# Seven block products for the feed-forward of two batches: attention and feed-forward on one Trainium2 core

## The chip, the core and the metric

The program runs on one core of one Trainium2 chip. A core has a matmul engine (PE in the profile; its weight loads PEld), a vector engine (DVE), a scalar engine (ACT), GpSimd (POOL) and a sequencer (SP) that issues the transfers here. The metric is device microseconds of one execution, lower is better. The kernel before takes 623.44 us, median of three runs (622.62 to 623.99).

## What is computed

Four batches of twelve heads, 448 positions of 64 values. Attention with capped scores, then two matrices with a gate between:

```
scores = cap * tanh((q @ k.T / 8) / cap);  attn = softmax(scores);  o = attn @ v
x = o.transpose(0, 2, 1, 3).reshape(1792, 768)
h = x @ w_in                                                  # 768 x 2048, float64 weights
g = where(h >= 1, h, where(h <= -1, 0, (h + 1)**2 / 4))
out = g @ w_out                                               # 2048 x 768
```

## The kernel before

`fast_body` holds the whole work; `general_body` behind it runs only if a verdict on the data's ranges, computed on the device, asks for it. Everything is kept transposed: model dimension on the 128 partitions, the 448 positions of one batch along the free axis.

A head pair (`attention(n)`, n from 0 to 23, six to a batch) is one unit of attention: `split` cuts q and k into two half-precision parts, `qk` multiplies the scores in three half-precision products, `expo` takes tanh and exp on the scalar engine, `add` sums exponentials on the vector engine, `av` multiplies with the values, `norm` and `divide` divide by the sums. For pairs 0 to 11 `av` runs in float32 (L444). For pairs from `HALVED` = 12 on, `halve` and `halve_v` (L385, L386, L391, L340) cut exponentials and values into two half-precision parts, and `av` runs three half-precision products (L433). How many of the four chunks of exponentials the vector engine sums and how many go to the matmul engine (L465) is `direct(n)`.

The feed-forward of a batch is two layers of 128x448 tiles. Layer one has 16 tiles of 6 chunks (`h_mm`, L537 to L539), layer two 6 tiles of 16 chunks (`o_mm`, L566 to L568). Each chunk is three half-precision matmuls: high weight by high data, low by high, high by low. Between the layers `h_out` applies the gate: two scalar-engine operations (L549, L550), a clamp on the vector engine (L551), and the cut into high and low half (L554, L555). The float64 weights come in 28 pieces; `piece` decodes each on the vector engine through one of two buffers `z` (L281 to L283) into float32 and then into two halves (L284 to L286). `piece_check` reads all pieces once more during batches 1 to 3 and reduces their largest and smallest magnitude (L297) for the verdict.

The order of all instructions is made at build time by `Plan`: every step is added with the buffers that it reads and writes, its possible engines and a cost; `order` then lists the steps on each engine by lateness in a planned schedule. The engines run their queues in that order and wait on semaphores. The steps of later attention pairs get a lead (`AHEAD`) and are planned among the feed-forward of the batches before; those of batch 3 lie among the feed-forward of batches 1 and 2.

## Time and profile before

| | |
|---|---|
| median of the runs | 623.44 us |
| the profiled execution, its time | 623.54 us |
| its span, first to last instruction | 621.7 us |
| PE busy | 607.5 us, 98% of the span |
| DVE busy | 427.8 us, 69% |
| ACT busy | 398.2 us, 64% |
| granted PE clock, mean | 0.997 of 2.4 GHz |
| moved by DMA | 74.6 MB, 120 GB/s on average |

Busy time is the time in which at least one instruction of an engine runs. Matmuls overlap each other, so the mean duration of one in a list is longer than the distance of two starts; the same holds, to a smaller degree, of the vector and the scalar engine. The granted clock is a share of 2.4 GHz; the lower of its two levels is 1.2 GHz. In the lists a group names line, engine, operation, what it writes and reads, its shape, then how often it occurs, its busy time in us and the mean ns of one, and behind the bar the engine's idle time before it and what ended that.

### The profile page before, as it was taken

How to read it: one execution, taken by the hardware profiler on the slowest of the kernel's cores; microseconds unless marked ns; L12 is line 12 of the kernel's file. 1: busy time of each engine (PE TensorE's matmuls, PEld its weight loads, DVE VectorE, ACT ScalarE, POOL GpSimd, SP SyncE). 2: the span in 40 equal slices, each digit the busy share in tenths (PEclk: the TensorE clock that was granted, in tenths of full speed). 3: DMA queues.
4: the chain of work that ended last, by engine and by line, in shares of the span. 5: the costliest groups of instructions: out<-in, count | busy, mean ns of one | idle time of the engine just before them, and what ended most of it. 6: DMA issues, size and time to landing. Idle time of an engine off the chain costs nothing.

```text
span 621.7 us, 8987 instructions
## 1 busy us (share of the span) xinstructions
PE 607.5 (98%) x3626; PEld 288.5 (46%) x3626; DVE 427.8 (69%) x673; ACT 398.2 (64%) x576; POOL 1.2 (0%) x6
## 2 busy tenths in 40 slices
PE   8998999999999999999999999999999999999995
PEld 2333454434445444444454444444545555555552
DVE  6997999999999569898875447888842105654200
ACT  7998977999845579897776459879622115551000
...
GB/s 344 310 260 167 185 67 179 172 142 169 199 208 97 98 33 113 107 133 117 152 116 129 65 40 52 58 102 74 129 134 31 15 31 102 101 137 146 36 16 34
DMA packets 18629, 74.60 MB, mean 120 GB/s; under 512 B 2066, under 2 KB 5266, under 8 KB 15506
## 3 DMA queue, kind: packets, MB, share of 16 engines
...
q14 instruction: 21, 0.17, 0.1%
q10 hardware_dynamic: 2, 0.00, 0.0%
...
## 4 chain that ended last, share of the span: by engine, by line
PE 71%; ACT 14%; DVE 11%; issue 2%; DMA 1%; POOL 0%; SPq 0%; DVEq 0%; ACTq 0%; POOLq 0%
PE f L566 12%; PE f L567 12%; PE f L568 12%; PE f L537 7%; PE f L538 7%; PE f L539 7%; PE s L367 5%; ACT e L375 4%; ACT e L377 4%; PE av L433 4%; PE av L444 2%; PE t L465 1%; DVE wr L551 1%; DVE spl L340 1%; DVE z L282 1%
## 5 line engine op out<-in xcount | busy, mean ns | idle before, releaser
L537 PE MATMUL f<-x,w 128*128 128x448 f16 x384 | 135.5, 353 | 1.5 <-DVE wr L551 1.5
L566 PE MATMUL f<-g,w 128*128 128x448 f16 x384 | 135.5, 353 | 0.1
L568 PE MATMUL f<-g,w 128*128 128x448 f16 x384 | 135.3, 352 | 0.0
L539 PE MATMUL f<-x,w 128*128 128x448 f16 x384 | 135.3, 352 | 0.0
L567 PE MATMUL f<-g,w 128*128 128x448 f16 x384 | 135.3, 352 | 0.0
L538 PE MATMUL f<-x,w 128*128 128x448 f16 x384 | 135.3, 352 | 0.0
L375 ACT ACTIVATE e<-s,tsc 128x896 f32<-128x896 f32 (+1 forms) x96 | 84.8, 902 | 9.6 <-PE s L367 8.6
L573 ACT ACTIVATE wr<-f 128x448 f32<-128x448 f32 x24 | 12.9, 538 | 100.3 <-PE f L568 100.3
L367 PE MATMUL s<-spl 64*128 64x448 f16 (+1 forms) x504 | 66.3, 352 | 0.6 <-DVE low L618 0.5
L297 DVE TENSOR_REDUCE chk<-raw 128x1 f32<-128x768 f32 (+1 forms) x56 | 58.0, 1060 | 10.9 <-DMA raw<-w_out 9.9
L537 PEld LDWEIGHTS <-w 128*128 128x128 f16 x384 | 37.5, 98 | 38.1 <-issue 4.4
L549 ACT ACTIVATE r<-f,half 128x448 f32<-128x448 f32 x64 | 40.2, 627 | 22.5 <-PE f L539 22.4
L554 ACT ACTIVATE g<-wr 128x448 f16<-128x448 f32 x64 | 36.6, 572 | 27.9 <-DVE wr L551 27.7
L566 PEld LDWEIGHTS <-w 128*128 128x128 f16 x384 | 37.5, 98 | 36.3 <-issue 2.2
L538 PEld LDWEIGHTS <-w 128*128 128x128 f16 x384 | 37.6, 98 | 35.7 <-issue 2.1
L568 PEld LDWEIGHTS <-w 128*128 128x128 f16 x384 | 37.6, 98 | 35.1
L539 PEld LDWEIGHTS <-w 128*128 128x128 f16 x384 | 37.6, 98 | 35.1
L567 PEld LDWEIGHTS <-w 128*128 128x128 f16 x384 | 37.6, 98 | 34.4 <-issue 0.3
L551 DVE SCALAR_TENSOR_TENSOR wr<-f,r 128x448 f32<-128x448 f32 x64 | 39.5, 619 | 18.2 <-ACT r L550 17.4
L377 ACT ACTIVATE e<-e,lnes,capb 128x896 f32<-128x896 f32 (+1 forms) x48 | 48.4, 1037 | 0.6
L555 DVE SCALAR_TENSOR_TENSOR g<-wr,g 128x448 f16<-128x448 f32 x64 | 39.4, 618 | 11.7 <-ACT g L554 11.4
L444 PE MATMUL av<-e,vt 128*64 128x448 f32 (+1 forms) x168 | 44.4, 562 | 1.0 <-ACT e L377 1.0
...
## 6 DMA issues: line engine op xcount, KB each, us to landing
...
vt<-vp SPq DMA_DIRECT2D x24, 256.0 KB, 3.1
...
```

The source lines that it names most:

```text
L297: dve(width, lambda j=j, op=op: V.tensor_reduce(out=chk[:, j:j + 1], in_=hi, op=op, axis=AX.X, apply_absolute_value=True), rk + after, [(" ...
L367: T.matmul(s[:, j, :S], lhsT=t[h, a, S + c * P:S + (c + 1) * P], rhs=t[h, b, :S], start=(i == 0), stop=(i == 2))
L375: act(w * S + 60, lambda: A.activation(e[:, :w], s[:, :w, :S], AF.Tanh, scale=tsc), sk + [("tsc", None)], ek)
L377: act(w * S + 110, lambda: A.activation(e[:, :w], e[:, :w], AF.Exp, scale=capb, **bias), ek + [("tsc", None)], ek)
L444: T.matmul(o, lhsT=w, rhs=m, start=(c == 0), stop=(c == 3))
L537: T.matmul(ph, lhsT=w1[:, 0, fc, c], rhs=x[c][0][:, 0], start=(c == 0), stop=False)
L538: T.matmul(ph, lhsT=w1[:, 1, fc, c], rhs=x[c][0][:, 0], start=False, stop=False)
L539: T.matmul(ph, lhsT=w1[:, 0, fc, c], rhs=x[c][0][:, 1], start=False, stop=(c == NCC - 1))
L551: dve(S, lambda: V.scalar_tensor_tensor(out=w, in0=ph, scalar=WS * XS, in1=r, op0=ALU.max, op1=ALU.min), fk + rk, wk)
L566: T.matmul(po, lhsT=hi[:, fc], rhs=gv[:, 0], start=(fc == 0), stop=False)
L567: T.matmul(po, lhsT=lo[:, fc], rhs=gv[:, 0], start=False, stop=False)
L568: T.matmul(po, lhsT=hi[:, fc], rhs=gv[:, 1], start=False, stop=(fc == NFC - 1))
```

## The change

The last two batches are taken together as two block columns of the data, and each layer's weights as 2x2 blocks (chunks by tiles). Both layers are multiplied with seven block products instead of eight (Strassen's scheme in its form with fifteen sums). For that:

- `attention` of all pairs comes before the two batches' feed-forward; pairs 18 to 23 (the last batch) use float32 values in `av` and are no longer halved.
- Decoded weights are kept in memory (`zd`); attended values of batches 2 and 3 (`xd`) and gated values of both batches (`gd`) are stored there in float32 and read back.
- `pair_up` loads four blocks and makes four differences, `halves_of` cuts each into two half-precision parts: 3 groups for layer one, 8 for layer two.
- `weights_sum` makes four sums of weight blocks, `weights_split` cuts them: 8 times for layer one (384 columns wide), 6 for layer two (512). Layer two's go over weights in place that are no longer needed.
- `product` is one block product; `copy_out` (scalar engine) and `plus` (vector engine) join products that two tiles share.
- The weight checks go through the `z` buffers in halves and are added to the plan behind the attention.

```diff
-HALVED = 2 * NPR
-ND = (B * NPR - HALVED) // 2
+HALVED = range(2 * NPR, 3 * NPR)
+PAIRED = 2 * NPR
+HF, HC, HE = NFC // 2, NCC // 2, NEC // 2
+STEP = 2
...
-WS, XS, GS, QS, ES = 2.0 ** 15, 2.0 ** 13, 4.0, 2.0 ** 10, 2.0 ** 5
+WS, XS, GS, QS, ES = 2.0 ** 13, 2.0 ** 13, 4.0, 2.0 ** 10, 2.0 ** 5
...
+    zd = [dr.tile([P, NCC * P if i < NP1 else NFC * EH], F32, name="zd%d" % i) for i in range(NT)]
+    xd = {n: dr.tile([P, S], F32, name="xd%d" % n) for n in range(PAIRED, B * NPR)}
+    gd = {(b, fc): dr.tile([P, S], F32, name="gd%d_%d" % (b, fc)) for b in (2, 3) for fc in range(NFC)}
...
+        dma(4 * P * width, lambda: M.dma_start(zd[i], z), zk, [("zd", i)])
...
-    def piece_check(i, after):
+    def piece_check(i, part):
 
         k = i - NP1
-        width = NCC * P if k < 0 else NFC * EH
-        t, rk = raws[6].bitcast(I32)[:, :2 * width], [(("w2", 6), None)]
+        width = (NCC * P if k < 0 else NFC * EH) // 2
+        zt, zk = take("z", zs)
+        t = zt.bitcast(I32)[:, :2 * width]
         hi = t.rearrange("p (n two) -> p n two", two=2)[:, :, 1].bitcast(F32)
-        src = w_in[i] if k < 0 else w_out[k]
-        dma(8 * P * width, lambda: M.dma_start(t, src.bitcast(I32)), [], rk)
-        for j, op in ((i, ALU.max), (NT + i, ALU.min)):
-            dve(width, lambda j=j, op=op: V.tensor_reduce(out=chk[:, j:j + 1], in_=hi, op=op, axis=AX.X, apply_absolute_value=True), rk + after, [("chk", j)])
+        src = (w_in[i] if k < 0 else w_out[k])[:, part * width:(part + 1) * width]
+        dma(8 * P * width, lambda: M.dma_start(t, src.bitcast(I32)), [], zk)
+        for j, op in ((0, ALU.max), (1, ALU.min)):
+            dve(width, lambda j=j, op=op: V.tensor_reduce(out=chp[:, j, i, part:part + 1], in_=hi, op=op, axis=AX.X, apply_absolute_value=True), zk, [("chp", (j, i, part))])
...
-            x, xk = st["x", n] = take_x()
-            xh, xl = [(xk, 0)], [(xk, 1)]
-            scale = XS if n < HALVED else 1.0
+            scale = 1.0 if n in HALVED else XS
             dve(S, lambda xf=xf, scale=scale: V.scalar_tensor_tensor(out=xf, in0=xf, scalar=scale, in1=t[:, :S], op0=ALU.mult, op1=ALU.mult), tk + fk, fk)
-            either(fk, xh, act_(S, lambda x=x, xf=xf: A.copy(x[:, 0], xf)), dve_(S, lambda x=x, xf=xf: V.tensor_copy(x[:, 0], xf), True))
-            left(S, x[:, 1], xf, 1.0, x[:, 0], FX + n, fk + xh, xl)
-
-    def take_x():
-
+            if n >= PAIRED:
+                dma(4 * P * S, lambda n=n, xf=xf: M.dma_start(xd[n], xf), fk, [("xd", n)])
+            if not 3 * NPR <= n < 3 * NPR + HC:
+                x, xk = st["x", n] = take_x(n)
+                halves_of(x, xk, xf, 1.0, fk, FX + n - (HC if n >= 3 * NPR else 0))
...
+    def halves_of(t, key, full, scale, r, j=None):
+
+        hk, lk = [(key, 0)], [(key, 1)]
+        cast = (lambda: A.copy(t[:, 0], full), lambda: V.tensor_copy(t[:, 0], full)) if scale == 1.0 else (lambda: A.activation(t[:, 0], full, AF.Copy, scale=scale), lambda: V.tensor_scalar(t[:, 0], full, scalar1=scale, scalar2=None, op0=ALU.mult))
+        either(r, hk, act_(S, cast[0]), dve_(S, cast[1], True))
+        if j is None:
+            dve(S, lambda: V.scalar_tensor_tensor(out=t[:, 1], in0=full, scalar=scale, in1=t[:, 0], op0=ALU.mult, op1=ALU.subtract), r + hk, lk)
+        else:
+            left(S, t[:, 1], full, scale, t[:, 0], j, r + hk, lk)
...
+    def gate(b, fc, src, key, dest, spill, keep):
+
+        (r, rk), (w, wk) = take("r", rs), dest
+        root = math.sqrt(GS)
+        acc = dict(accum_out=racc[:, b]) if fc == 0 else {}
+        act(S + (170 if acc else 0), lambda: A.activation(r, src, AF.Relu, bias=half, scale=0.5 * root / (WS * XS), **acc), key + [("half", None)], rk + [(("racc", b), fc)])
+        act(S, lambda: A.activation(r, r, AF.Square, scale=math.sqrt(WS * XS / GS)), rk, rk)
+        dve(S, lambda: V.scalar_tensor_tensor(out=w, in0=src, scalar=WS * XS, in1=r, op0=ALU.max, op1=ALU.min), key + rk, wk)
+        if spill:
+            dma(4 * P * S, lambda: M.dma_start(gd[b, fc], w), wk, [("gd", (b, fc))])
+        if keep is not None:
+            t, gk = st["g", b, fc] = keep
+            halves_of(t, gk, w, GS / (WS * XS), wk)
...
-    pieces = [lambda a, i=i: piece_check(i, a) for i in range(NT)]
-    checks = [(), pieces[::3], pieces[1::3], pieces[2::3]]
-    for b in range(B):
+    for b in range(2):
...
-        if b < B - 1:
-            for n in range(NPR):
-                plan.lead, plan.held = AHEAD * (b > 0), b > 0
-                attention((b + 1) * NPR + n)
-                plan.lead, plan.held = 0.0, False
+        for n in range((b + 1) * NPR, (b + 2 + b) * NPR):
+            plan.lead, plan.held = AHEAD[n // NPR - 1], b > 0
+            attention(n)
+            plan.lead, plan.held = 0.0, False
...
+    for i in range(NT):
+        for part in range(2):
+            piece_check(i, part)
...
+    def pair_up(srcs):
+
+        tiles = [take_from("xl", xl, xlk) for _ in srcs]
+        for (dram, dk), (t, k) in zip(srcs, tiles):
+            dma(4 * P * S, lambda t=t, dram=dram: M.dma_start(t, dram), [dk], k)
+        (a, ak), (d, dk), (e, ek), (b, bk) = tiles
+        less = lambda out, x, y, r, w: dve(S, lambda: V.tensor_tensor(out=out, in0=x, in1=y, op=ALU.subtract), r, w)
+        less(a, d, a, ak + dk, ak)
+        less(d, e, d, ek + dk, dk)
+        less(e, e, a, ek + ak, ek)
+        less(b, b, e, bk + ek, bk)
+        return [(a, ak), (e, ek), (d, dk), (b, bk)]
...
+    def product(bank, first, stop, lhs, rhs, r):
+
+        t, k = bank
+        n = len(rhs)
+
+        def run():
+            for c in range(n):
+                for i, (x, y) in enumerate(((0, 0), (1, 0), (0, 1))):
+                    T.matmul(t, lhsT=lhs(x, c), rhs=rhs[c][0][:, y], start=(first and c == i == 0), stop=(stop and c == n - 1 and i == 2), skip_group_check=True)
+        pe(567 * n, run, r + [(key, j) for _, key in rhs for j in range(2)] + ([] if first else k), k)
...
+    def weights_sum(a11, a12, a21, a22, keys, n):
+
+        k11, k12, k21, k22 = keys
+        tt = lambda out, x, y, op, r, w: dve(n, lambda: V.tensor_tensor(out=out, in0=x, in1=y, op=op), r, w)
+        tt(a22, a21, a22, ALU.add, k21 + k22, k22)
+        tt(a21, a11, a21, ALU.subtract, k11 + k21, k21)
+        tt(a11, a22, a11, ALU.subtract, k11 + k22, k11)
+        tt(a12, a12, a11, ALU.subtract, k11 + k12, k12)
+
+    def weights_split(n, hi, lo, full, r, hk, lk):
+        either(r, hk, act_(n, lambda: A.activation(hi, full, AF.Copy, scale=-WS)), dve_(n, lambda: V.tensor_scalar(hi, full, scalar1=-WS, scalar2=None, op0=ALU.mult), True))
+        dve(n, lambda: V.scalar_tensor_tensor(out=lo, in0=full, scalar=-WS, in1=hi, op0=ALU.mult, op1=ALU.subtract), r + hk, lk)
...
+    half1 = HC * P
+    for i in range(HF):
+        (za, zak), (zb, zbk) = take_from("zl", zl, zlk), take_from("zl", zl, zlk)
+        for t, k, src in ((za, zak, i), (zb, zbk, HF + i)):
+            dma(4 * P * NCC * P, lambda t=t, src=src: M.dma_start(t, zd[src]), [("zd", src)], k)
+        part = lambda k: [[(k[0][0], q)] for q in range(2)]
+        (k11, k12), (k21, k22) = part(zak), part(zbk)
+        weights_sum(za[:, :half1], za[:, half1:], zb[:, :half1], zb[:, half1:], (k11, k12, k21, k22), half1)
...
+        y, x, z = new_bank(), new_bank(), new_bank()
+        product(y, True, True, wl(i, 0), xb(PAIRED), wk(i))
+        p1 = copy_out(y)
+        product(x, True, True, wl(i, HC), xb(PAIRED + HC), wk(i))
+        plus(x, p1)
+        gate(2, i, *p1, p1, True, keep_g())
+        product(y, False, True, sl(sa, 0), tb(1), sak)
+        u2 = copy_out(y)
+        product(z, True, True, sl(sb_, 0), tb(2), sbk)
+        product(y, False, True, sl(sb_, HC), tb(0), sbk)
+        u4 = copy_out(y)
+        product(y, False, True, sl(sa, HC), xb(3 * NPR + HC), sak)
+        gate(3, i, *y, take_from("u", us, uk), True, None)
+        plus(z, u4)
+        gate(3, HF + i, *u4, u4, True, keep_g())
+        product(z, False, True, wl(HF + i, HC), tb(3), wk(HF + i))
+        plus(z, u2)
+        gate(2, HF + i, *u2, u2, True, keep_g())
...
+            if i < 4:
+                pair_g(done)
+                done += 1
...
+    p1s, u2s, u4s = [], [], []
+    for i in range(HE):
+        steps(ys[i], True, wv(i, 0), ga(2, 0), wqk(i, 0))
+        p1s.append(scaled(ys[i]))
+    for i in range(HE):
+        steps(xbs[i], True, wv(i, 1), ga(2, 1), wqk(i, 1))
+        plus(xbs[i], p1s[i], out_scale)
+        store(2, i, p1s[i])
+    while done < HF:
+        pair_g(done)
+        done += 1
...
+    for i in range(HE):
+        for h in range(2):
+            tiles = [take_from("zl2", zl2, zl2k) for _ in range(4)]
+            for q, (t, k) in enumerate(tiles):
+                src = zd[NP1 + 2 * (i + q // 2 * HE) + h][:, q % 2 * HF * EH:(q % 2 + 1) * HF * EH]
+                dma(4 * P * HF * EH, lambda t=t, src=src: M.dma_start(t, src), [("zd", NP1 + 2 * (i + q // 2 * HE) + h)], k)
+            weights_sum(*[t for t, _ in tiles], [k for _, k in tiles], HF * EH)
...
+            dests = [([s2v[i][j][:, :, e] for j in range(2)], ("s2", i))]
+            dests += [([w2_half(ec, j)[:, f * HF:(f + 1) * HF, e] for j in range(2)], ("wq", ec, f)) for ec, f in ((i, 1), (i, 0), (HE + i, 0))]
+            for (d, dk), (t, k) in zip(dests, tiles):
+                weights_split(HF * EH, d[0], d[1], t.rearrange("p (f e) -> p f e", e=EH), k, [(dk, (h, 0))], [(dk, (h, 1))])
+    for i in range(HE):
+        steps(wbs[i], True, wv(i, 1), ga(3, 1), wqk(i, 1))
+    for i in range(HE):
+        steps(ys[i], False, lambda x, c, i=i: s2v[i][x][:, c], gb(1), [(("s2", i), None)])
+        u2s.append(scaled(ys[i]))
+    for i in range(HE):
+        steps(ys[i], False, wv(HE + i, 0), gb(0), wqk(HE + i, 0))
+        u4s.append(scaled(ys[i]))
+        c12 = take_from("xl", xl, xlk)
+        plus(wbs[i], u4s[i], out_scale, c12)
+        store(3, i, c12)
+    for i in range(HE):
+        steps(zbs[i], True, wv(i, 0), gb(2), wqk(i, 0))
+        plus(zbs[i], u4s[i], out_scale)
+        store(3, HE + i, u4s[i])
+        steps(zbs[i], False, wv(HE + i, 1), gb(3), wqk(HE + i, 1))
+        plus(zbs[i], u2s[i], out_scale)
+        store(2, HE + i, u2s[i])
```

How the order moves, in three places. Names are the program's buffers: `t0` is the PSUM bank of sums, `rr0` their reciprocals, `e0` to `e4` exponentials and later weights, `xf` attended values, `eh0`, `vh0`, `vh1` the blocks of `pair_up`, `qkr`, `spl` q and k and later weight sums, `w2_2` layer-two weights of tile 2, `chk`, `chp` check results.

First place: the vector engine at the last reciprocal of the attention (pair 23). Before:

```order
L475 RECIPROCAL rr0_129<-t0_142 128x224
L386 TENSOR_TENSOR eh0_99<-e2_96,eh0_99 128x896
L478 SCALAR_TENSOR_TENSOR mix0_130<-mix0_130,low_73,rr0_129 128x224
L297 TENSOR_REDUCE chk_76<-raw_85 128x1 x2
L482 TENSOR_REDUCE chk_76<-rr0_129 128x1 x2
L386 TENSOR_TENSOR z0_86<-e3_97,z0_86 128x896
L494 SCALAR_TENSOR_TENSOR xf0_131<-xf0_131,t0_142 128x448
L386 TENSOR_TENSOR z1_87<-e4_98,z1_87 128x896
L340 SCALAR_TENSOR_TENSOR x1_106,fin_74<-xf0_131,x1_106 128x448
L386 TENSOR_TENSOR eh0_99<-e0_94,eh0_99 128x448
```

Now:

```order
L489 RECIPROCAL rr0_132<-t0_145 128x224
L307 TENSOR_REDUCE chp_80<-z1_90 128x1
L492 SCALAR_TENSOR_TENSOR mix0_133<-mix0_133,low_75,rr0_132 128x224
L307 TENSOR_REDUCE chp_80<-z1_90 128x1
L331 MEMSET rr0_132 1x71
L506 SCALAR_TENSOR_TENSOR xf0_134<-xf0_134,t0_145 128x448
L307 TENSOR_REDUCE chp_80<-z0_89 128x1
L354 SCALAR_TENSOR_TENSOR e0_97,fin_76<-eh0_102,e0_97 128x448
L354 SCALAR_TENSOR_TENSOR x1_109,fin_76<-xf0_134,x1_109 128x448
L354 SCALAR_TENSOR_TENSOR e0_97,fin_76<-vh1_104,e0_97 128x448
```

Between the reciprocal and the two attended values of the last pairs there were halves of exponentials; now there are halves of block differences (`e0`, from `eh0` and `vh1`) and weight checks, and the second attended value, `xf1`, stands 17 rows behind the first.

Second place: the vector engine some forty instructions later, at the third block group of layer one (`sums0` and `sums1` now hold halves of differences):

```order
L781 SCALAR_TENSOR_TENSOR spl1_94<-e4_101,spl1_94 128x768
L735 TENSOR_TENSOR eh0_102<-eh0_102 128x448
L773 TENSOR_TENSOR e3_100<-e3_100 128x384
L735 TENSOR_TENSOR eh0_102<-vh0_103,eh0_102 128x448
L354 SCALAR_TENSOR_TENSOR sums0_106,fin_76<-eh0_102,sums0_106 128x448
L735 TENSOR_TENSOR vh0_103<-vh0_103,eh0_102 128x448
L354 SCALAR_TENSOR_TENSOR sums1_107,fin_76<-eh0_102,sums1_107 128x448
L781 SCALAR_TENSOR_TENSOR spl0_93<-e3_100,spl0_93 128x768
```

and the matmul engine at the product that reads `sums1`:

```order
L758 LDWEIGHTS qkr1_92
L758 MATMUL s0_140<-e2_99,qkr1_92 128x448
L758 LDWEIGHTS qkr1_92
L758 MATMUL s0_140<-sums1_107,qkr1_92 128x448
L758 LDWEIGHTS qkr1_92
...
L758 LDWEIGHTS qkr0_91
L758 MATMUL f0_142<-x4_112,qkr0_91 128x448
```

This is the first product of a block difference. Nothing of it was in the old order, where the feed-forward of batch 3 needed batch 3 alone.

Third place: the vector engine at the last group of layer-two weight sums, where `w2_2` is written over:

```order
L773 TENSOR_TENSOR spl1_94<-spl0_93,spl1_94 128x512
L768 SCALAR_TENSOR_TENSOR xf1_135<-s1_141,xf1_135 128x448
L773 TENSOR_TENSOR spl0_93<-qkr0_91,spl0_93 128x512
L307 TENSOR_REDUCE chp_80<-z0_89 128x1
L773 TENSOR_TENSOR qkr0_91<-spl1_94,qkr0_91 128x512
L307 TENSOR_REDUCE chp_80<-z0_89 128x1
L773 TENSOR_TENSOR qkr1_92<-qkr1_92,qkr0_91 128x512
L307 TENSOR_REDUCE chp_80<-z1_90 128x1 x2
L781 SCALAR_TENSOR_TENSOR w2_2_84<-qkr1_92,w2_2_84 128x8x64
L781 SCALAR_TENSOR_TENSOR w1_81<-qkr0_91,w1_81 128x8x64
L781 SCALAR_TENSOR_TENSOR w2_5_87<-spl1_94,w2_5_87 128x8x64
```

and the matmul engine at the product that reads the new `w2_2` into bank `s0`, the third tile of that block product:

```order
L758 LDWEIGHTS w2_4_86
L758 MATMUL f1_143<-raw_88,w2_4_86 128x448
L758 LDWEIGHTS w2_4_86
L758 MATMUL f1_143<-raw_88,w2_4_86 128x448
L758 LDWEIGHTS w2_2_84
L758 MATMUL s0_140<-g16_131,w2_2_84 128x448
```

In the old order weights were written once, in the first third of the program; now the second layer's are written again while its products run.

## Rows read from the trace of the kernel before

**Rows 1.** Windows of stretches: busy us (instructions) of each engine, granted clock, DMA share.

```profile
core 0: us, PE busy (x) PEld busy (x) DVE busy (x) ACT busy (x) POOL busy (x), PEclk, DMA share, GB/s
62.00:200.00 138.00, 137.63 (x826) 63.19 (x826) 134.61 (x184) 114.25 (x161) 0.00 (x0) 1.00 0.46 159
200.00:424.00 224.00, 222.23 (x1368) 107.66 (x1366) 164.98 (x244) 168.56 (x244) 0.00 (x0) 1.00 0.28 92
424.00:615.00 191.00, 190.48 (x1039) 97.22 (x1037) 74.95 (x126) 60.92 (x103) 0.59 (x1) 1.00 0.22 78
615.00:621.70 6.70, 0.01 (x1) 0.00 (x0) 0.00 (x0) 0.54 (x1) 0.00 (x0) 0.69 0.13 42
```

**Rows 2.** The page, part 1: busy us of each engine, share of the span.

```profile
PE 607.5 (98%) x3626; PEld 288.5 (46%) x3626; DVE 427.8 (69%) x673; ACT 398.2 (64%) x576; POOL 1.2 (0%) x6
```

**Rows 3.** Groups of instructions by line and form, feed-forward matmuls.

```profile
L537 PE MATMUL f<-x,w 128*128 128x448 f16 x384 | 135.5, 353 | 1.5 <-DVE wr L551 1.5
...
L566 PE MATMUL f<-g,w 128*128 128x448 f16 x384 | 135.5, 353 | 0.1
```

**Rows 4.** Timeline of the matmul engine near the end: start us, us.

```profile
600.09 0.35 PE L566 MATMUL f<-g,w 128*128 128x448 f16 x1
600.28 0.35 PE L567 MATMUL f<-g,w 128*128 128x448 f16 x1
```

**Rows 5.** The chain that ended last: start us, us, float32 and halved products of values, sums.

```profile
35.24 2.52 PE av L444 x12
37.76 1.27 PE t L465 x24
...
304.62 1.25 PE av L433 x12
...
308.01 1.36 PE av L433 x9
```

**Rows 6.** Timeline of the vector engine in its full stretch: start us, us.

```profile
68.47 0.62 DVE L551 SCALAR_TENSOR_TENSOR wr<-f,r 128x448 f32<-128x448 f32 x1
69.01 0.62 DVE L555 SCALAR_TENSOR_TENSOR g<-wr,g 128x448 f16<-128x448 f32 x1
69.54 0.55 DVE L281 TENSOR_SCALAR z<-w 128x768 int32<-128x768 int32 x1
70.01 0.95 DVE L286 SCALAR_TENSOR_TENSOR w<-z,w 128x768 f16<-128x768 f32 x1
70.88 0.95 DVE L282 SCALAR_TENSOR_TENSOR z<-w,z 128x768 int32<-128x768 int32 x1
```

**Rows 7.** Groups by line and form, vector engine: shapes, count, busy us, mean ns.

```profile
L555 DVE SCALAR_TENSOR_TENSOR g<-wr,g 128x448 f16<-128x448 f32 x64 | 39.4, 618 | 11.7 <-ACT g L554 11.4
...
L405 DVE TENSOR_TENSOR sums<-e,e 128x896 f32<-128x896 f32 x24 | 26.1, 1087 | 14.2 <-ACT e L377 14.1
...
L475 DVE RECIPROCAL rr<-t 128x224 f32<-128x224 f32 x12 | 18.6, 1551 | 7.1 <-PE t L465 7.1
...
L286 DVE SCALAR_TENSOR_TENSOR w<-z,w 128x768 f16<-128x768 f32 x16 | 15.0, 945 | 0.0
...
L413 DVE TENSOR_TENSOR sums<-sums,e 64x448 f32<-64x448 f32 x24 | 14.8, 618 | 2.0 <-ACT e L377 1.7
...
L340 DVE SCALAR_TENSOR_TENSOR vh<-vt,vh 128x512 f16<-128x512 f32 x12 | 8.2, 680 | 0.1
```

**Rows 8.** Groups by line and form, scalar engine.

```profile
L554 ACT ACTIVATE g<-wr 128x448 f16<-128x448 f32 x64 | 36.6, 572 | 27.9 <-DVE wr L551 27.7
...
L573 ACT ACTIVATE wr<-f 128x448 f32<-128x448 f32 x24 | 12.9, 538 | 100.3 <-PE f L568 100.3
```

**Rows 9.** Transfers: a 256 KB load on the page, and line L574, its 224 KB stores.

```profile
vt<-vp SPq DMA_DIRECT2D x24, 256.0 KB, 3.1
...
DMA to landing us min/median/max: 1.9/2.0/4.3
```

**Rows 10.** Timeline of the end: last matmul, its scaling, its store.

```profile
614.65 0.35 PE L568 MATMUL f<-g,w 128*128 128x448 f16 x1
615.09 0.54 ACT L573 ACTIVATE wr<-f 128x448 f32<-128x448 f32 x1 [8.54 <-PE f L568]
615.66 0.33 SPq L574 DMA_DIRECT2D out<-wr  x1
```

**Rows 11.** Timeline of the start: the warming matmuls, eight of one shape.

```profile
3.36 3.17 PE L590 MATMUL f<-x 128*128 128x448 f16 x8
...
L590 PE MATMUL f<-x 128*128 128x448 f16 x12 | 4.8, 575 | 1.2 <-POOL x L584 1.2
```

190 lines of the change are left out of this document (152 added, 38 removed).

## The prediction, made before the change was run

> **What bounds the kernel now.** The sum is made against the profiled execution: 623.5 us, of which 621.7 are the span and 1.8 lie around it; the median of the three runs is 623.4, so the two agree within 0.2, and 0.2% of it, 1.2 us, is about what a measurement of this kernel can tell from no change. I read the windows first [rows 1]. From 62 us to 615 us the matmul engine is busy in 550.3 of 553 us at the full granted clock, so its work sets the end; the page's busy times say the same [rows 2]. The reader should see a second thing in rows 1: from 62 to 200 us the vector engine is busy in 134.6 of 138 us, 97.5%, and the matmul engine still loses nothing, while from 424 us on it is busy in only 75 of 191. The change spends that idle time. Busy matmul time is not matmul work: a record lasts 353 ns [rows 3], but in a steady stretch one starts every 0.19 us [rows 4]; over 448 columns that is 448/2.4 = 187 ns. I price all 128x448 half-precision matmuls so.
>
> **Matmuls removed.** The feed-forward has six lines of 384 matmuls, of which two stand in [rows 3], 2304 in all and 1152 for the last two batches. With seven products layer one needs 8 steps x 7 products x 3 chunks x 3 = 504, layer two 3 x 7 x 8 x 3 = 504: 1008. So 144 x 0.187 = 26.9 us go.
>
> **Matmuls added.** Pairs 18 to 23 multiply values in float32. Of the halved form, 12 records of two chunks take 1.25 us and the other two chunks 1.36; of the float32 form, 12 records (three chunks of two heads) take 2.52 [rows 5]. From start to start, the halved form has 12 steps of 0.187, 2.24 us a pair of heads, the float32 one four chunks of 0.75 to 0.79, 3.0 to 3.15: six pairs add 4.5 to 5.5 us; I take 4.5, the steps at full rate. The fourth chunk's sums move to the matmul engine: three chunks take 1.27 us there [rows 5], so six more take about 2.2 from start to start. Matmul work: -26.9 + 4.5 + 2.2 = **-20.2 us** (-18 to -21). If nothing waits, the time is 603.3.
>
> **What the vector engine gets.** Its instructions overlap: a 448-element one lasts 0.62 us, the next starts 0.53 to 0.54 later, a 768-element one lasts 0.95 and gives way after 0.87 [rows 6]. So from each mean [rows 7] I take off 0.08: 0.54 for 448 elements (subtractions of both kinds, clamps, halves, sums from PSUM), 0.60 for 512, 0.87 for 768, 1.47 for the reciprocal. The 384-element sums are not in the trace; between the 448-element row and nothing, by the slope of 448 to 896, they come to 0.47 (0.4 to 0.54). Over the whole kernel the change removes the halving of e and v of six pairs and some sums (about -37 us) and adds pair differences with their halves, weight sums with theirs and the joining of products (about +125): 428 becomes some 515 us. On average that fits. It is not spread evenly: block differences need both batches' values, so nothing of them can start before the last attention pair, and the layer-two weights can only be overwritten late.
>
> I therefore count one stretch in the new order: from the last reciprocal of the attention to the last weight half that the matmul engine needs for the third tile of its layer-two product with bank s (order rows of the third place). The vector engine has 285 instructions there: 165 of 448 elements x 0.54 = 88.7 (39 subtractions, 41 + 24 low halves, 32 clamps, 26 joins and three more), 32 of 384 x 0.47 = 15.0, 44 of 512 x 0.60 = 26.5, 16 of 768 x 0.87 = 13.9, 24 half-width weight checks at 0.47 to 0.60 = 14.0, and 2 us of small ones: **160.0 us**. The matmul engine has 783 half-precision matmuls, 7 float32 ones and 4 spreads between the same two points: 146.2 + 3.0 + 0.4, less what overlaps the reciprocal's own wait: **149.3 us**. Even if the vector engine never pauses, the matmul engine waits 10.7 us in this stretch. About half of it comes at once: up to the low half of `sums1` (second place) the vector engine has 43 instructions, 23.7 us, the matmul engine 18.3. Behind that low half on the vector engine stand the first weights of the next step, and behind the waiting product stand all others, the queue being in order.
>
> The vector engine will pause, too. In its fullest stretch before it was 97.5% busy [rows 1]; at that share 160.0 becomes 164.1 and the wait **14.8 us**. Bounds: 10.7 (no pause) and, at 90%, 28.5. I take 97.5% since this is the nearest row: the same planner with the same kind of mix. After this point the vector engine has 27 us of work, mostly checks that nothing waits for, against 42.6 us of matmuls: no further wait.
>
> **What I cost at nothing.** The scalar engine gets about 24 copies, 44 casts and 40 weight halves at 0.45 to 0.65 each and loses as many of the halving: 398 becomes about 430 of a span of 616 [rows 2, 8]; cover is that it is busy in only 61 of 191 us after 424 us [rows 1]. The 28 stores of decoded weights (up to 512 KB) fall into the first 200 us, where the DMA engines are 46% busy after 62 us; each holds one of the two z buffers longer. A 224 KB store takes 2.0 us, 4.3 at worst [rows 9]; a piece uses a z buffer for five vector instructions, 4 us, and two buffers alternate, so a hold of 3 to 5 us is covered; without that cover it is 0 to 3 us. The checks only move. At the end the last matmul is followed, as before, by one join and one store [rows 10]; the verdict's small operations stand just ahead of that join, within the 4.5 us of the last product: 0 to 1 us.
>
> **The sum.** 623.5 - 20.2 + 14.8 = **618.1 us**.
>
> **Rivals.** *The vector engine does not pace the matmul engine* (chance 0.08). For: it has run full without a loss [rows 1]. Against: these are chains, and the count gives the order's own minimum. If only the first wait is real: 603.3 + 5.4 = 608.7.
>
> *Waits for memory* (0.17), the slower side. Eleven groups of four blocks and fourteen of weights go out to memory and come back, and the in-order vector engine subtracts them as they land: 25 places where it can stop while its whole queue stands behind. For: a 256 KB load has a median of 3.1 us and a 224 KB store goes from 1.9 to 4.3 [rows 9], and a ring of four blocks lets one group load at a time. Against: the queue holds other ready work between, some 5 us a group. With half a microsecond each, 25 x 0.5 = 12.5 more, 630.6. It decides from 0.22 us a group on: 5.4 us more make the gain nothing. The Trainium skill, "DMA: Bandwidth & Descriptors", section "Latency and other measured facts", gives memory access as a fraction of a microsecond on average and 2 us at high load; by that, loads in this stretch would swing by more than the price above, and the worst store of rows 9 agrees, being 2.4 us over the best.
>
> *The matmul clock falls in the waits* (0.13). Before, after its last matmul at 615 us, the granted clock of the last 6.7 us is 0.69 on average [rows 1], so it does drop in a pause; the matmuls at the very start took 575 ns and stood 0.37 us apart, twice the later 0.19 [rows 11], which is 1.2 instead of 2.4 GHz. Twelve such cost 2.2 us. A wait of 5 us in one piece, which the old kernel never has, could cost that once, two of them twice: 620.3 to 622.5. The Trainium skill, "TensorE: Matmul & The Clock Gate", section "HAM oscillation — how this bites in real kernels", says that waits between bursts of matmuls put the array back to the slow clock; by that rule it would be 620.3, and rows 1 agree as far as they go.
>
> *The change does not do what it says* (0.02): the verdict sends the program into the general body, whose whole second pass would put it far above 700 us. The new limits (the largest attended value between 1/16 and 2) lie wide around values of this data.
>
> **How the numbers follow.** Forecast 0.60, rivals 0.08, 0.17, 0.13, 0.02. The likeliest is 618.1. The forecast's own range is 612 (no pause) to 624. The whole range, 608 to 630, takes in the first rival's half, the clock and the nearer half of the memory waits, and leaves out about 0.15. Faster by over 0.2% (below 622.2): 0.58 + 0.08 + 0.07 = 0.73; within: 0.10; slower (above 624.7): 0.17.
>
> **What would show it.** Right: 1008 matmuls on the product's line; the vector engine over 95% busy for some 160 us after the last attention pair; matmul waits of 10 to 18 us in that stretch, put down to the vector engine's subtractions and low halves; a first wait near 5 us at the product that reads `sums1`; a quiet last 40 us. Wrong: vector waits of over 6 us there put down to loads (memory), a granted clock below 1.00 in the stretch (clock), matmul losses before the last attention pair (the stores of weights), or a matmul engine without waits.

## The result, and the profile after

The changed kernel takes **629.06 us** (median of four runs, 628.04 to 629.29) against 623.03 of the kernel before: ratio 1.0093, 95% interval 1.0074 to 1.0112. It is slower; 618.1 was forecast. The profiled execution took 629.3, of which 627.4 are the span.

The page of the changed kernel, part 1, which answers to [rows 2]:

```profile
PE 593.9 (95%) x3488; PEld 276.6 (44%) x3488; DVE 518.4 (83%) x929; ACT 424.2 (68%) x640; POOL 1.2 (0%) x6
```

The vector engine's 518.4 us (515 forecast) and the scalar engine's 424.2 (430) are what was counted. The matmul engine is busy for 13.6 us less than before and the kernel takes 6 us more, so the question is where it waits. Windows after the last reciprocal (402.4 us), columns as in [rows 1]:

```profile
400.00:420.00 20.00, 20.00 (x128) 10.13 (x128) 19.23 (x42) 9.85 (x19) 0.00 (x0) 1.00 0.79 259
420.00:440.00 20.00, 14.39 (x66) 6.73 (x65) 18.73 (x41) 9.54 (x17) 0.00 (x0) 0.83 0.62 185
440.00:460.00 20.00, 18.70 (x98) 9.38 (x96) 17.67 (x33) 17.36 (x34) 0.00 (x0) 1.00 0.70 222
460.00:480.00 20.00, 18.36 (x97) 9.33 (x96) 19.29 (x35) 17.85 (x34) 0.00 (x0) 1.00 0.49 171
480.00:500.00 20.00, 18.98 (x100) 9.61 (x99) 18.47 (x38) 15.95 (x29) 0.00 (x0) 1.00 0.57 179
500.00:520.00 20.00, 18.07 (x94) 8.97 (x92) 17.67 (x40) 13.37 (x26) 0.00 (x0) 1.00 0.68 219
520.00:540.00 20.00, 20.00 (x108) 10.35 (x106) 20.00 (x46) 12.54 (x24) 0.00 (x0) 1.00 0.72 217
540.00:560.00 20.00, 19.83 (x106) 10.08 (x105) 19.96 (x43) 10.24 (x18) 0.00 (x0) 1.00 0.69 219
560.00:580.00 20.00, 17.14 (x84) 8.30 (x83) 19.66 (x39) 7.02 (x13) 0.00 (x0) 0.91 0.63 208
```

Three things stand there: a hole in 420 to 440 us and a smaller one in 560 to 580, both with a lower granted clock, and from 440 to 520 us a loss of 1 to 2 us in each window, at the full clock, while the vector engine is busy in 17.7 to 19.3 of 20. The waits of the matmul engine from 400 to 625 us (in total, times, longest) name them:

```profile
PE s L758 <- ACT sums L516: 5.6, 1, 5.6
PE f L758 <- ACT sums L516: 2.4, 1, 2.4
PE s L758 <- DVE vt L768: 2.3, 3, 1.2
PE s L758 <- ACT vt L763: 2.1, 4, 0.8
PE f L758 <- ACT vt L763: 1.2, 1, 1.2
PE s L758 <- ACT wr L763: 1.1, 2, 0.6
PE s L758 <- DVE r L768: 0.7, 1, 0.7
PE f L758 <- DVE sums L354: 0.5, 1, 0.5
```

L516 and L354 make the halves of block differences; L763 copies a bank out and L768 joins a product to such a copy. The first row is the wait that the prediction put at 5.4. The rows of L763 and L768 it did not have at all: in them a product waits to continue in a bank that is still being read. One from the timeline, matmul, scalar and vector engine:

```profile
440.65 0.73 PE L758 MATMUL s<-sums,spl 128*128 128x448 f16 x3
440.68 0.58 ACT L584 ACTIVATE r<-r 128x448 f32<-128x448 f32 x1
441.17 0.65 ACT L583 ACTIVATE r<-wr,half 128x448 f32<-128x448 f32 x1
441.34 0.62 DVE L585 SCALAR_TENSOR_TENSOR xf<-f,r 128x448 f32<-128x448 f32 x1
441.85 0.58 ACT L584 ACTIVATE r<-r 128x448 f32<-128x448 f32 x1
441.88 1.15 DVE L768 SCALAR_TENSOR_TENSOR vt<-s,vt 128x448 f32<-128x448 f32 x2
442.55 1.29 PE L758 MATMUL s<-x,spl 128*128 128x448 f16 x6 [1.16 <-DVE vt L768]
```

The join at 441.88 stands in the vector queue behind a clamp (L585), which needs the scalar engine's square (L584, until 441.26). Clamp and join each start 0.53 us after the instruction ahead of them, so the vector engine runs without a pause here; the last matmul had ended at 441.38, 0.50 ahead of the join, and the next product starts when the join ends. An earlier clamp did wait 0.59 us for its square (at 438.80). On the scalar engine an instruction that does not need the one ahead follows the square after 0.49 us (440.68 to 441.17), and the square that needs the one ahead follows it after 0.68 (441.17 to 441.85). Part of this is the kind of instruction: behind L583, one that does not need it starts 0.52 to 0.58 us later (13 times in this trace), the square that does 0.64 to 0.70 (43 times).

**Where the time went.** Take from the end of the last matmul the work of all matmuls up to it, each at its price of the prediction. Before: 615.0 - 569.3 = 45.7 us not used; after: 619.8 - 549.2 = 70.6. So the work fell by 20.1 and the losses rose by 24.9. The prices are the prediction's own; the 20.1 confirms how many matmuls there are, not what each costs. Cut at the first score matmul of pair 23, they rose by 2.8 ahead of it (40.7 to 43.5) and by **22.2** behind it (4.9 to 27.1). In the product's own line starts lie 0.189 us apart when nothing waits. Of its 1008 matmuls 18 start later because of a wait, 19.6 us together: 5.8 at the first wait, 3.2 at the two of layer two, 10.6 at 15 short ones, nearly all at copies and joins. Another 18 start 0.37 us apart, 3.3 us in all, at the half clock after the two holes (granted 0.50 from 424 to 430 us). Behind the last matmul come 7.6 us instead of 6.7.

### The profile page after: what moved, and what is told of

The parts are those of the page before. It is cut to its first block, busy times and chain, and to the rows that moved or that the text cites. A ratio compares the mean times of both kernels' runs of the same rounds, so it can differ in the third digit from the quotient of the medians.

```text
span 627.4 us, 9468 instructions
## 1 busy us (share of the span) xinstructions
PE 593.9 (95%) x3488; PEld 276.6 (44%) x3488; DVE 518.4 (83%) x929; ACT 424.2 (68%) x640; POOL 1.2 (0%) x6
## 4 chain that ended last, share of the span: by engine, by line
PE 37%; DVE 27%; ACT 21%; DMA 7%; issue 6%; SPq 0%; POOL 0%; DVEq 0%; ACTq 0%; POOLq 0%
ACT e L389 5%; PE av L458 5%; PE s L381 4%; ACT e L391 4%; PE s L758 4%; PE f L573 3%; PE f L574 3%; PE f L575 3%; PE f L609 3%; PE f L611 3%; PE f L610 3%; DMA zd<-z 2%; ACT r L583 2%; DMA z<-w_out 2%; DVE z L291 2%
## 5 line engine op out<-in xcount | busy, mean ns | idle before, releaser
L758 PEld LDWEIGHTS <-w 128*128 128x128 f16 x720 | 70.6, 98 | 73.2 <-issue 8.6
L389 ACT ACTIVATE e<-s,tsc 128x896 f32<-128x896 f32 (+1 forms) x96 | 85.0, 905 | 15.4 <-PE s L381 12.5
L307 DVE TENSOR_REDUCE chp<-z 128x1 f32<-128x384 f32 (+1 forms) x112 | 63.6, 604 | 30.5 <-DMA z<-w_in 18.9
L573 PE MATMUL f<-x,w 128*128 128x448 f16 x192 | 67.8, 353 | 2.7 <-DVE wr L585 1.7
L575 PE MATMUL f<-x,w 128*128 128x448 f16 x192 | 67.7, 352 | 0.3 <-DVE x L354 0.3
L391 ACT ACTIVATE e<-e,capb 128x896 f32<-128x896 f32 x72 | 67.0, 948 | 1.4
L609 PE MATMUL f<-g,w 128*128 128x448 f16 x192 | 67.8, 353 | 0.0
L611 PE MATMUL f<-g,w 128*128 128x448 f16 x192 | 67.7, 352 | 0.0
L610 PE MATMUL f<-g,w 128*128 128x448 f16 x192 | 67.7, 352 | 0.0
L574 PE MATMUL f<-x,w 128*128 128x448 f16 x192 | 67.7, 352 | 0.0
L419 DVE TENSOR_TENSOR sums<-e,e 128x896 f32<-128x896 f32 x24 | 26.1, 1089 | 14.9 <-ACT e L391 14.5
L584 ACT ACTIVATE r<-r 128x448 f32<-128x448 f32 x64 | 36.9, 576 | 1.5
L354 DVE SCALAR_TENSOR_TENSOR spl<-qkr,spl 128x960 f16<-128x960 f32 (+2 forms) x25 | 27.8, 1112 | 4.6 <-ACT spl L366 3.2
L295 DVE SCALAR_TENSOR_TENSOR w<-z,w 128x768 f16<-128x768 f32 (+1 forms) x28 | 29.9, 1068 | 2.0 <-ACT w L294 1.8
L294 ACT ACTIVATE w<-z 128x768 f16<-128x768 f32 (+1 forms) x24 | 22.7, 947 | 11.9 <-DVE z L291 11.8
L573 PEld LDWEIGHTS <-w 128*128 128x128 f16 x192 | 18.8, 98 | 20.8 <-issue 4.5
L574 PEld LDWEIGHTS <-w 128*128 128x128 f16 x192 | 18.8, 98 | 20.4 <-issue 4.5
L609 PEld LDWEIGHTS <-w 128*128 128x128 f16 x192 | 18.8, 98 | 19.8 <-issue 3.4
```

Of the source, the lines that this page charges most:

```text
L307: dve(width, lambda j=j, op=op: V.tensor_reduce(out=chp[:, j, i, part:part + 1], in_=hi, op=op, axis=AX.X, apply_absolute_value=True), zk, ...
L389: act(w * S + 60, lambda: A.activation(e[:, :w], s[:, :w, :S], AF.Tanh, scale=tsc), sk + [("tsc", None)], ek)
L391: act(w * S + 110, lambda: A.activation(e[:, :w], e[:, :w], AF.Exp, scale=capb, **bias), ek + [("tsc", None)], ek)
L573: T.matmul(ph, lhsT=w1[:, 0, fc, c], rhs=x[c][0][:, 0], start=(c == 0), stop=False)
L574: T.matmul(ph, lhsT=w1[:, 1, fc, c], rhs=x[c][0][:, 0], start=False, stop=False)
L575: T.matmul(ph, lhsT=w1[:, 0, fc, c], rhs=x[c][0][:, 1], start=False, stop=(c == NCC - 1))
```

## Experiments

Each time stands against the kernel before, timed beside it (medians of 622.5 to 623.4); the ratio's interval is given where it decides. In the four runs without sums, checks, joins or stores the verdict gets a constant, so that the fast body stays the one that runs.

**The block sums left out** (`less` and `tt` do nothing).

```diff
-    less = lambda ...: dve(S, lambda: V.tensor_tensor(out=out, in0=x, in1=y, op=ALU.subtract), r, w)
+    less = lambda ...: dve(S, lambda: None, r, w)
```

> The changed kernel in its own order, with the subtractions and additions of blocks left out: those of the values (L735) and of the weights (L773). Everything else stays, the loads and the halves too, so the products get plain blocks and the output is not the reference's. The vector engine loses 39 x 0.54 + 32 x 0.47 + 24 x 0.60 = 50 us in the stretch from the last reciprocal to the layer-two weights, where it has 160. Theory (the vector engine's work in the stretch paces the matmuls): the matmul waits after the last attention pair fall from 22 us to under 8 (the waits of layer one on copies and joins may stay), time 610 to 616 instead of 629. Rival (round trips through memory): loads, stores and their order stay, so the waits stay, 626 to 629.

619.52 (ratio 0.9947, 0.9925 to 0.9969): a gain of 9.5, less than expected; the losses behind pair 23 are 15.8, where less than 8 was expected. With 50 us less in the vector queue the first wait is still 2.5 us, the second is gone, and most of the waits on L763 and L768 are as they were (the trace is that of the fastest of its eight runs, 616.5):

```profile
PE s L758 <- ACT sums L516: 2.5, 1, 2.5
PE s L758 <- DVE vt L768: 2.5, 3, 1.2
PE s L758 <- ACT vt L763: 1.9, 4, 0.8
```

**The weight checks left out, their loads kept.**

```diff
-            dve(width, lambda ...: V.tensor_reduce(out=chp[:, j, i, part:part + 1], in_=hi, ...), zk, ...)
+            dve(width, lambda: None, zk, ...)
```

> The changed kernel in its own order, with the vector engine's weight checks (L307) left out, their loads kept; the verdict gets a constant in their place. 24 of the checks, 14 us, stand in the stretch after the last reciprocal. Theory (vector work paces): the 160 us become 146, less than the 149 of the matmul engine, so most of the wait that is not chain latency goes: 10 to 14 us less, 615 to 619. Rival (memory): the traffic is the same, 627 to 629. Rival (the checks only fill gaps in which the vector engine waits anyway): 626 to 629, with vector gaps where the checks stood.

626.77 (ratio 1.0061, 1.0041 to 1.0082): 14 us less vector work bought 2.3. The rival of the gaps holds. In 400 to 440 us the vector engine is now busy in only 30 of 40, and the same two waits are 4.7 and 2.0 instead of 5.6 and 2.4. Behind 400 us the vector engine now waits longer at joins for a product, first in the changed kernel, then here:

```profile
DVE vt L768 <- PE s L758: 3.3, 3, 1.7
...
DVE vt L768 <- PE s L758: 16.4, 4, 6.7
```

So most of the checks stood where the vector engine would have waited anyway, and work there does not count.

**Idle matmuls in the long waits.** `product` gets a count of matmuls with zero weights ahead of one of its chunks.

```diff
+                if rhs[c][1] == at:
+                    idle(t, count, xs[3][:, 0])
```

> The changed kernel with matmuls that change nothing (zero weights, accumulated) put into the two longest waits of the matmul engine: 28 ahead of the one that reads sums1 (5.6 us of wait), 12 ahead of the layer-two one that reads sums0 (2.4 us). If they keep the clock up, the granted clock of 420 to 440 us goes from 0.83 to 1.00 and that of 560 to 580 from 0.91 to 1.00. Theory (the lowered clock costs some 3 us beside the waits): 625.5 to 627. Rival (the vector engine paces again right after, so time won there is waited away later): 628.5 to 629.5, with a later wait that is longer by the gain.

635.38. The first 28 had been put into the wrong product, one that does not wait: they cost their own 5.3 us, and the hole stayed (6.2 us). It says nothing on the price of the clock there.

> As the run before with idle matmuls of zero weights, but the first 29 now stand in the product of the second bank s, just ahead of its matmuls that read sums1, where the matmul engine waits 5.6 us; the other 12 as before. The granted clock of 420 to 440 us should be 1.00 instead of 0.83, that of 560 to 580 us 1.00 instead of 0.91. Theory (18 matmuls at half speed cost 3.3 us of the end): 625.5 to 627. Rival (the vector engine and the joins pace after each wait, so the time won is waited away): 628 to 629.5.

629.47 (ratio 1.0118, 1.0089 to 1.0146). The rival holds. The granted clock is 1.00 in both windows,

```profile
420.00:440.00 20.00, 18.58 (x97) 9.24 (x96) 19.46 (x41) 10.09 (x19) 0.00 (x0) 1.00 0.64 188
560.00:580.00 20.00, 18.79 (x99) 9.39 (x97) 19.86 (x39) 6.31 (x11) 0.00 (x0) 1.00 0.69 216
```

but the next join starts the matmuls again at 441.86 instead of 442.55. Of 3.3 us at the half clock 0.7 come back. The medians of the spans agree (626.6 instead of 627.2 us); the time gains nothing, since this kernel takes 2.3 to 3.3 us outside its span, where the changed kernel takes 1.8 to 1.9.

**Loads issued twice.**

```diff
-        dma(4 * P * S, lambda ...: M.dma_start(t, dram), [dk], k)
+        dma(4 * P * S, lambda ...: (M.dma_start(t, dram), M.dma_start(t, dram)), [dk], k)
```

> The changed kernel with each load of the block groups (values, gates, weights) issued twice, the second over the first, so that the data stand 1 to 3 us later and the traffic of loads in the tail doubles. Theory (vector work paces, loads are covered): 629 to 631. Rival (round trips through memory hold up the vector queue): 25 groups later by half a microsecond or more each, 640 or more, with vector waits put down to loads.

806.78, far outside both. Each second load waited in SP's queue until the first into the same buffer had landed, and the queue behind it waited too. These waits are new:

```profile
SPq L812 <- DMA e<-zd: 54.8, 16, 6.2
SPq L733 <- DMA vh<-gd: 43.6, 16, 3.6
SPq L733 <- DMA eh<-gd: 42.4, 16, 3.3
SPq L898 <- DMA spl<-zd: 24.1, 8, 5.2
```

They come to 165 us; 178 were lost. It tested the queue, not the round trips; these are judged from the trace of the change below.

**Layer one without copies and joins.**

```diff
-        act(S, (lambda: A.copy(u, t)) if scale == 1.0 else ..., k, ukey)
+        act(S, lambda: None, k, ukey)
```

> The changed kernel in its own order, without the copies out of the banks (L763) and the joins of products (L768) in layer one, so its gates work on old data and the output is not the reference's. The matmul engine then never waits for a bank that is still being read. Theory (the waits of 0.4 to 1.2 us in layer one, some 7 us in all, are the latency from the last matmul of a product over copy and join to the next product in the same bank): 440 to 520 us free of waits, 620 to 623. Rival (they are the vector engine's backlog; 14 us of its work less act as the checks left out did): 625 to 627, the short waits still there.

620.54 (ratio 0.9973, 0.9956 to 0.9991), as the theory said. The matmul engine is full where it lost 5.9 us:

```profile
440.00:460.00 20.00, 19.95 (x107) 10.16 (x105) 16.13 (x29) 16.93 (x29) 0.00 (x0) 1.00 0.68 219
460.00:480.00 20.00, 20.00 (x108) 10.32 (x107) 17.56 (x33) 17.19 (x31) 0.00 (x0) 1.00 0.60 207
480.00:500.00 20.00, 20.00 (x107) 10.36 (x106) 18.61 (x41) 14.75 (x27) 0.00 (x0) 1.00 0.71 216
500.00:520.00 20.00, 20.00 (x108) 10.37 (x106) 18.14 (x40) 14.42 (x27) 0.00 (x0) 1.00 0.78 244
```

The first wait is untouched (5.4). So the short waits are those of copy and join, and without both the end comes 8.5 us earlier. The 14 us of vector work that go with them are not the reason: 14 us of checks were worth 2.3.

**One layer at a time.** Layer one plain, without `pair_up` of values and weight sums, and layer two plain, without `pair_g` and weight sums:

```diff
+        for b, f in ((2, i), (3, i), (3, HF + i), (2, HF + i)):
+            y = new_bank()
+            product(y, True, True, lambda x, c, f=f: w1[:, x, f, c], [st["x", b * NPR + k] for k in range(NCC)], ...)
+            gate(b, f, *y, take_from("u", us, uk), True, ...)
```

```diff
+            for c0 in range(0, NFC, STEP):
+                product(y, c0 == 0, c0 + STEP == NFC, lambda x, c, ...: w2_half(ec, x)[:, c0 + c], gs[c0:c0 + STEP], wkey)
+            store(b, ec, scaled(y))
```

> Layer one of the last two batches plain again (576 matmuls in place of 504, no block differences of the values, no joins, no sums of its weights, 16 of the 28 weight stores gone); layer two stays the block product. Matmul work is 13.5 us more than in the change. Theory (most of the waits sit in layer one: the first wait of 5.6, its half-speed matmuls 2.3, the short waits of some 7, some of the front's 2.8): 15 to 17 us of waits go, 625 to 628, and from 400 to 520 us the matmul engine is busy without a break. Rival (the vector engine's total work paces, 55 us of it are gone): all 22 us of waits in the tail go, 619 to 622.

> Layer one as block product, layer two of the last two batches plain again (576 matmuls in place of 504, no gate differences, no sums of its weights, no reloads of them). Matmul work is 13.5 us more than in the change. Theory (the waits sit in layer one): only the second wait of 2.9 us with its clock of 1 us and the short waits at the end of 2 go, 635 to 638. Rival (total vector work paces, some 95 us of it are gone after the attention): 619 to 623.

629.68 with layer two alone as block product, 641.43 with layer one alone, both slower than theory and rival had it. (In the first, eight values share seven x buffers, so pair 12's are overwritten by pair 23's; the work is the full one.) The second has 452.9 us of vector work instead of 518.4, and the matmul engine still loses 1.0 to 2.6 us in every window from 440 to 520 us: the rival of total vector work falls. Set against 629.06, the block product of layer two is worth 12.4 us beside that of layer one, and that of layer one 0.6 beside that of layer two, where each takes away 13.5 us of matmuls. These are differences of whole orders, each planned anew, and not the worth of a layer: the matmul engine loses 5.4 us from 350 to 420 us in the first and 4.9 from 250 to 300 us in the second. Against the kernel before with the float32 values (628.39, below), layer two alone is 1.3 us slower and layer one alone 13.0. No run has both layers plain with all attention ahead, so what that order costs by itself is not shown.

**Stores of weights left out, all but two.**

```diff
-        dma(4 * P * width, lambda: M.dma_start(zd[i], z), zk, [("zd", i)])
+        dma(4 * P * width, (lambda: M.dma_start(zd[i], z)) if i in (0, NP1) else lambda: None, zk, [("zd", i)])
```

> The changed kernel in its own order with 26 of the 28 weight stores left out; one of each size stays, and all reloads read these two, so the output is not the reference's. Theory (the matmul engine's 2.8 us more of losses before the last attention pair come from z buffers held by the stores): the waits near 70 and 211 us go, 626 to 627. Rival (they are the new order's): 628.5 to 629.5.

630.57 (ratio 1.0124, 1.0086 to 1.0163). The wait at 70 us (1.3) is there, but two at 211 and 213 us (1.0 and 0.9) are gone, and pair 23 starts 3.0 us earlier (381.9 instead of 384.9). About 1 of these 3 us lies in the first 10 us, where traces of one order differ as much; the other 2 are the stores'. The trace of the changed kernel shows how: a half of exponentials (L399) goes into a `z` buffer and waits for the store out of it to end.

```profile
208.55 0.94 ACT L399 CAST z<-e 128x896 f16<-128x896 f32 x1 [7.76 <-DMA zd<-z]
...
211.77 0.73 PE L381 MATMUL s<-spl 128*128 128x448 f16 x3 [1.00 <-ACT e L389]
```

The time did not fall all the same: in this trace 0.7 us more are lost behind pair 23, and 9.7 us follow the last matmul instead of 7.6, for a reason that is not shown; the four runs lie between 628.0 and 632.8.

**Float32 values alone, in the kernel before.**

```diff
-HALVED = 2 * NPR
+HALVED = range(2 * NPR, 3 * NPR)
```

> The kernel before with one part of the change alone: pairs 18 to 23 multiply their values in float32, the feed-forward stays plain. The matmul engine gets 4.5 us for the values and 2.2 for the sums of the fourth chunk, the vector engine loses 37 us. Theory (matmul work sets the end, vector work has slack): 623 + 6.7 = 629 to 631. Rival (the vector engine held something up there): 623 to 626.

628.39 (ratio 1.0076, 1.0059 to 1.0093), just below what the theory had. At the prediction's prices the work rose by 6.8 and the losses fell by 1.4; whether the price is high or less was lost, this does not tell. The part that the block product needs costs 5.0 us of time.

**The same instructions in another order.** Two figures of the planner's table:

```diff
-       ("ACT", "DVE"): 33, ("ACT", "ACT"): 0,
+       ("ACT", "DVE"): 140, ("ACT", "ACT"): 180,
```

> The changed kernel's instructions in another order: the planner's table of delays between dependent instructions gets 180 ns in place of 0 from scalar engine to scalar engine and 140 in place of 33 from scalar to vector engine, as the trace of the changed kernel has them; nothing else is edited. Theory (the short waits of layer one are chains of gate, copy and join that the order was laid out too tight for): the waits of 0.4 to 1.2 us between 440 and 520 us shrink from some 5 us to under 2, 619 to 624. Rival (they are inherent in continuing in the bank that was just copied): 627 to 629.

**620.42** (ratio 0.9943, 0.9922 to 0.9964), faster than the kernel before, with the same instructions. The time is as expected, its reason only in part: the waits over 0.4 us between 440 and 520 us went only from 5.0 to 3.6; the larger part is the first hole, 1.3 us now, with no half clock behind it:

```profile
420.00:440.00 20.00, 18.16 (x94) 9.04 (x93) 18.23 (x38) 12.17 (x24) 0.00 (x0) 1.00 0.62 191
```

The vector work of the whole stretch is the same in this kernel, so it does not set the first wait. The count up to the waiting product does, if it is made on the new order. Counted alike, at the prediction's prices, from the last reciprocal to the first product that reads a difference in `sums`, the changed kernel has 23.2 us of vector work against 17.8 of matmuls, this one 24.5 against 23.7. The excess falls from 5.4 to 0.8 us, the matmul engine's loss up to there from 6.5 to 2.0.

**Sums on GpSimd**, with these delays.

```diff
-    less = lambda out, x, y, r, w: dve(S, lambda: V.tensor_tensor(...), r, w)
+    less = lambda out, x, y, r, w: pool(105 + S / 1.1, lambda: G.tensor_tensor(...), r, w)
```

> As the run with the other delays, and the 100 block sums of values, gates and weights (L735, L773) on GpSimd, which has nothing else to do, instead of the vector engine. Theory (the sums stand in the vector queue ahead of joins and halves that the matmul engine waits for; leaving them out gave 619.5): 612 to 619, below the kernel before. Rival (GpSimd takes longer for each, or holds up vector instructions meanwhile, so the chains to the first and second long wait grow): 625 or more, with the first wait over 6 us.

667.45. GpSimd takes 1.2 to 1.5 us on average (its spans are rough) for what the vector engine does in 0.55 to 0.62, though 1.13 and 1.00 where no vector instruction overlaps it, and vector instructions with two inputs from SBUF stretch meanwhile, which the checks, with one input, do not (three in 1.86):

```profile
415.25 1.39 POOL L735 TENSOR_TENSOR vh<-vh,vh 128x448 f32<-128x448 f32 x1
416.61 1.37 POOL L773 TENSOR_TENSOR e<-e 128x384 f32<-128x384 f32 x1
...
414.11 0.61 DVE L768 SCALAR_TENSOR_TENSOR wr<-s,wr 128x448 f32<-128x448 f32 x1
...
417.06 1.41 DVE L354 SCALAR_TENSOR_TENSOR sums<-vh,sums 128x448 f16<-128x448 f32 x1
...
419.74 1.86 DVE L307 TENSOR_REDUCE chp<-z 128x1 f32<-128x512 f32 x3
```

The Trainium skill, "SBUF — State Buffer", section "🔬 SBUF: two separate sides", says that such a vector instruction and a GpSimd one that reads SBUF shut each other out for a whole instruction. The 1.41 instead of 0.62 agrees.

**Both kernels with better figures.**

> The kernel before, with the two delays of the planner's table as in the run with the other delays (180 and 140 ns). Theory (the table matters where products wait for copies and joins, which the old kernel does not have; its matmul engine waits 3 us in all after 62 us): 621 to 624. Rival (the table lays out any of these orders better, and the block product has no part in the 620.4): 613 to 618.

> The changed kernel with the two delays, and the attention of batches two and three drawn forward by 30 and 45 us in the planner instead of 20 and 30, so that more plain matmuls of batch one are left beside the block differences. Theory (what remains is the wait for sums and joins, which plain matmuls cover): 616 to 620. Rival (the remaining waits lie in layer two and at the end, where no plain matmul is left): 619 to 622.

> The changed kernel with the two delays, and the planner's figure for a load or store from issue to landing raised by half a microsecond; in the trace loads of 224 KB land after 3.7 to 4.1 us, the planner has 2.8. Theory (vector queue entries placed too early for their loads cost something in the tail): 616 to 620. Rival (loads are covered): 619 to 622.

> The kernel before with both edits of the planner's figures that gave the block product 614.5: the two delays, and half a microsecond more until a load lands. Theory (the old kernel's loads are covered by plain matmuls): 617 to 619, as with the delays alone, so that the block product is 3 to 5 us faster than the plain one, each laid out with its better figures. Rival (the figure helps any order): 613 to 615, and the block product is no gain at all.

> The changed kernel with the two delays, the later landing and the attention of batch three drawn forward by 35 us instead of 30. Theory (the two gains overlap, both come from the tail): 612 to 616. Rival (they add up): 608 to 611.

The edits beside the two delays:

```diff
-AHEAD = 0.0, 20000.0, 30000.0
+AHEAD = 0.0, 30000.0, 45000.0
-        sp = lambda i: 2000 + self.steps[i][2] / RATE
+        sp = lambda i: 2500 + self.steps[i][2] / RATE
```

In the last one AHEAD ends in 20000.0, 35000.0.

| kernel | figures | us | ratio to before, interval |
|---|---|---|---|
| before | two delays | 617.98 | 0.9923, 0.9906 to 0.9939 |
| before | and loads later | 618.52 | 0.9924, 0.9907 to 0.9940 |
| changed | two delays | 620.42 | 0.9943, 0.9922 to 0.9964 |
| changed | and more drawn forward | 614.60 | 0.9864, 0.9848 to 0.9881 |
| changed | and loads later | 614.49 | 0.9877, 0.9850 to 0.9905 |
| changed | all three | **611.46** | 0.9815, 0.9797 to 0.9832 |

The delays help the plain kernel, too, by 4.5 us (its losses fall from 45.7 to 41.1, mostly ahead of pair 23), as the rival said and the theory did not. The later loads add nothing to it, as expected; to the changed kernel they and the earlier attention each give 6 us, more than expected. Together, with a smaller step of the attention, they give 9, a little more than the theory and less than the rival had. At the best of the figures tried, the block product is 1.1% faster (0.9815 / 0.9923); the earlier attention was not tried in the kernel before. In the fastest kernel the longest wait, 2.6 us, is one for the layer-two weights, and there the vector engine is full:

```profile
500.00:520.00 20.00, 20.00 (x107) 10.37 (x106) 20.00 (x46) 13.42 (x25) 0.00 (x0) 1.00 0.74 229
520.00:540.00 20.00, 16.68 (x87) 8.27 (x85) 20.00 (x43) 9.71 (x17) 0.00 (x0) 0.98 0.67 211
```

Later loads in the planner move the whole order, so its 5.9 us do not show that loads were late. Part of what makes the other orders better can be counted as above, now from the last reciprocal to the first product of layer two that reads a difference in `sums`:

| changed kernel | vector work over matmul work, us | matmul engine's loss, us |
|---|---|---|
| as it was | 11.3 | 21.6 |
| two delays | 5.4 | 14.3 |
| and more drawn forward | -3.4 | 9.2 |
| and loads later | 0.8 | 8.6 |
| all three | 7.0 | 12.5 |

The better orders put 6 to 25 us more matmuls into this stretch, beside 0 to 10 us more vector work. In every row 5 to 13 us are lost beyond the excess.

## Why the prediction was wrong

The time lay inside the whole range of 608 to 630, but a gain of 5.3 us was forecast and a loss of 6.0 measured.

- **Matmul work, -20.2: right as a count.** The trace has the matmuls that were counted, and in the product's line they start 0.189 us apart (0.187 taken). The price of the float32 values is less sure: 6.7 us of work was taken, and made alone they added 5.0 us of time.
- **Vector work in the stretch, 160.0 us: right as a count.** From 402 to 573 us the vector engine is busy for 161.9, at 94.7% instead of 97.5.
- **The wait of 14.8 us: the step that failed.** It was 22.2, and these 7.4 us are the largest part of the 11 that were missed. "At that share 160.0 becomes 164.1 and the wait 14.8" treats the vector work as one block of time. It is a queue in order, which stops at a join until its product is ready, and for which the matmul engine stops in turn. Only the waits for sums are of the forecast kind, 9.0 us (5.8, 5.4 forecast, and 3.2). Beside them stand 10.6 us of 15 short waits, nearly all at copies and joins, which the text had costed as vector and scalar time alone; three of them lie in the last 40 us, which were to be quiet. The count without a share, 10.7, was a floor, and it held. The layer-one kernel and the checks left out show that vector work in total does not set what comes above it; the kernel without joins shows what the sum lacked.
- **The stores of weights, "0 to 3 us", put at nothing in the sum.** The losses ahead of pair 23 rose by 2.8, and some 2 of them go with the stores. The cover did not hold: not the next piece but a half of exponentials waited for the buffer, 7.8 us. The end cost 0.9, inside its bounds.
- **"The vector engine does not pace the matmul engine"** was to give 603.3 to 608.7 us; with 50 us less vector work the kernel took 619.5, since the joins remain.
- **Waits for memory: not here.** From 402 to 573 us vector waits on loads come to 0.7 us in two rows:

```profile
DVE chp L307 <- DMA z<-w_out: 0.5, 1, 0.5
...
DVE e L773 <- DMA e<-zd: 0.2, 1, 0.2
```

The rival's time, 630.6, came near 629.1 by luck.
- **The matmul clock: it fell, as rows 1 and 11 let expect, and cost almost nothing.** 18 matmuls ran at 1.2 GHz, 3.3 us, but the next join held the engine up until nearly the same moment: 0.7 us came back without it. The price, read at the start of the old kernel where nothing held the matmuls up, does not hold ahead of a join.
- **The order was taken as given.** The prediction priced the work of the new order and never asked whether the planner's delays fit a kernel full of short chains. Two figures there are worth 8.6 us (4.5 in the kernel before), all are worth 17.6.
